# Start-up of a polynomial-attention and MLP kernel: batch 0's keys in three loads, constants, fillers and weight conversion in another order

## The chip, the cores and the metric

One core of a Trainium2 chip. The metric is the device time of one execution in microseconds (us), the median of the runs. The engines are TensorE (PE, with PEld for its weight loads), VectorE (DVE), ScalarE (ACT), GpSimd (POOL) and SyncE (SP), which only issues DMAs here.

## The reference

```
phi(x)  = outer(S1 x, S2 x), 8 x 8 features       # per batch, head and position
kv = sum over positions of phi(k) v ; z = sum over positions of phi(k)
attn = (phi(q) kv) / (phi(q) z + 1e-6)            # batch 4, 4 heads, 1088 positions, 32 wide
x = attn with the heads side by side              # 4 x 1088 rows of 128
xn = (x - mean(x)) / sqrt(var(x) + 1e-6) * g_ln
out = x + relu(xn W1) W2                          # W1 128 x 512, W2 512 x 128
```

q, k and v are float32. S1, S2, W1 and W2 arrive as float64, and the kernel turns them into float32 itself.

## The kernel before

The kernel's order is written out by hand: each engine works through its own queue in the order of the calls, and waits on semaphores for what it needs. The four batches pass through the stages keys (`turn_k`, `key_features`, `key_products`, `key_sums`, `key_scale`, `key_values`, `key_spread`), queries (`turn_q`, `query_features`, `query_rows`, `quotients`, `query_products`, `query_turn`), numerators (`numerators`, `columns_of`) and the MLP (`hidden`, `second`, `finish`, with `stats` and `root` for the norm), each batch's MLP under the next batch's attention. The rows of the output are in nine chunks; the first two are batch 0's halves.

The change is in the start-up, in which batch 0's first half passes alone while the weights are converted. These parts of it matter:

- **Loads.** `load_rows` (L94) issues one DMA on SP for a batch's keys or queries, 128 partitions with 34 positions of 32 floats each. SP's order at the start is S2, batch 0's keys (`kn`), queries (`qn`), W1, four loads of v, W2. VectorE's `turn_k(0, 0, 4, 0, 4)` turns the keys of the first four of nine position tiles of each group, two more calls the others.
- **Constants on GpSimd.** Ahead of everything: zeros in `vn` (L113), two iotas, the identity, `ident8` (L144), zeros in both `kT` (L148), -0.5 in `mhalf` (L150, the exponent of the norm's root), 1e-6 in `ac` (L155), zeros in `sq` (L159).
- **S.** L179 to L208: VectorE takes the float64 words of S1 and S2 apart and puts float32 together in `s_f`; `sketches` makes the projection matrices from it on TensorE.
- **Weight conversion.** Class `weight`: `split` (VectorE, L179 and L181, exponent and upper mantissa bits), `floats` on ScalarE (step 0 and 1: exponent, L242 and L244; step 2: mantissa, L246; step 3: low word, L248), `add` (GpSimd, L265, mantissa plus low word), `signed` (VectorE, L185), `last` (VectorE, L273, the product). For W2, `exps` (VectorE, L253 and L255) stands in place of steps 0 and 1. W1 is converted in halves of 256 columns; `split` writes both halves into the PSUM banks M[0] and M[2]. Each converted half goes through `mean_free` on TensorE, and a copy (L658 or L672) brings it back as `w1`.
- **Fillers.** `fill(n, bank, w)` (L161) has TensorE multiply ones by ones, n times w columns, with nothing that reads the result.

The order of the conversion among the rest, before:

```
W1.split(0, half); key_products ...; W1.split(half, half)
query_features(0, 0, 4) ... W1.floats ... quotients(0, 0, 4); key_values(0)
query_products, query_turn; W1.add(0, half); W1.add(half, half)
W1.signed(0, half); W1.last(dve, 0, half); W1.signed(half, half); W2.floats(3)
numerators(0, 0, 4); mean_free(0, M[0]); W1.last(dve, half, half)
turn_q(0, 4, 4); W2.split(); W2.exps(); W2.signed(); hidden(0, 0)
query_features(0, 4, 4); mean_free(half, FB); hidden(0, 1); W2.floats(2); W2.add()
query_rows(0, 4, 4); W2.last(dve); turn_k(1, ...)
```

Of the kernel before, what the change touches and what calls it, by code (L numbers as in the profile page):

```python
# [16 lines left out]
def _ap(t: bass.AP, p0: int, np_: int, off: int, free, step: int = 1):  # L17

    p = list(t.ap)[0]
    return bass.AP(  # L20
        t.tensor, t.offset + p0 * p[0] + off, [[p[0] * step, np_]] + [list(d) for d in free]
    )
# [3 lines left out]
def kernel(  # L26
# [20 lines left out]
    P = 128  # L47
# [24 lines left out]
    def const(shape, dtype, name):  # L72
        return consts.tile(shape, dtype, name=name)
# [17 lines left out]
    w1_raw = const([P, DH], moe_w_ch1.dtype, "w1_raw")  # L91
    w2_raw = const([P, JC * DM], moe_w_ch2.dtype, "w2_raw")

    def load_rows(dst, src, b):  # L94
        nc.sync.dma_start(
            out=dst[b],
            in_=bass.AP(src.tensor, src.offset + b * H * S * D, [[G * D, P], [1, G * D]]),
        )

    def load_v(b):  # L100
        base = v.offset + b * H * S * D
        for r in range(4):
# [4 lines left out]
                in_=bass.AP(v.tensor, base + NT * D * r, [[G * D, 32], [S * D, H], [1, n]]),  # L107
            )


    dve.memset(_ap(vn[0], 0, P, 7 * D, [[VH, H], [1, 2 * D]]), 0.0)
    for b in range(1, B):
        pool.memset(_ap(vn[b], 96, 32, 7 * D, [[VH, H], [1, 2 * D]]), 0.0)  # L113
    load_rows(kn, k, 0)
    load_rows(qn, q, 0)
    nc.sync.dma_start(out=w1_raw, in_=moe_w_ch1)
    load_v(0)
# [23 lines left out]
                      op0=ALU.logical_shift_right, op1=ALU.bitwise_and)  # L141
    dve.tensor_tensor(out=m8, in0=bit, in1=head, op=ALU.is_equal)
    ident8 = const([R2, P], F32, "ident8")
    pool.tensor_copy(out=_ap(ident8, 0, R2, 0, [[R, 16], [1, R]]),  # L144
                     in_=_ap(ident, 0, R2, R, [[0, 16], [1, R]]))
    kT = [const([P, NT * P], F32, f"kT{i}") for i in range(2)]
    for t in kT:
        pool.memset(t[:, 7 * P :], 0.0)  # L148
    mhalf = const([P, 4], F32, "mhalf")
    pool.memset(mhalf, -0.5)  # L150

    NE = R + 1
    acs = [const([P, 32 * NE], F32, f"ac{i}") for i in range(2)]
    for t in acs:
        pool.memset(_ap(t, 0, P, R, [[NE, 32]]), 1e-6)  # L155

    sq = [const([P, 32], F32, f"sq{b}") for b in range(B)]
    for t in sq:
        pool.memset(t, 0.0)  # L159

    def fill(n, bank, w=P):  # L161
        for _ in range(n):
            pe.matmul(bank[:, 0:w], ones, _ap(ones, 0, P, 0, [[0, w // P], [1, P]]),  # L163
                      start=True, stop=True)
# [52 lines left out]
    class weight:  # L217


        def __init__(self, dst, raw, tag, banks=None):  # L220
            self.dst, self.raw, self.plain = dst, raw, raw.dtype == F32
            self.banks = banks
            if not self.plain:
                self.t = exponent(raw, P, raw.shape[-1], tag)

        def cols(self, a, n):
            t = {k: x[:, a : a + n] for k, x in self.t.items()}
            if self.banks:

                y = self.banks[a // n].bitcast(U32)  # L230
                t["ex"], t["bits"] = y[:, 0:n], y[:, n : 2 * n]
            return t

# [38 lines left out]
                t = self.cols(a, n)  # L272
                eng.tensor_tensor(out=dst, in0=t["mant"], in1=t["e3"].bitcast(F32), op=ALU.mult)  # L273

    W1 = weight(w1g, w1_raw, "w1", banks=(M[0], M[2]))
    W2 = weight(w2, w2_raw, "w2")


# [14 lines left out]
    def sketches(y):  # L293

        pe.matmul(y[:, P : P + R2], s_f, ident[0:R2, 0:R2], start=True, stop=True)
        dve.tensor_tensor(
            out=_ap(sk, 0, P, 0, [[HR, 2], [R, H], [1, R]]),
            in0=_ap(y, 0, P, P, [[R, 2], [0, H], [1, R]]),
            in1=_ap(m32, 0, P, 0, [[0, 2], [1, H], [0, R]]),
            op=ALU.mult,  # L300
        )
        act.copy(sq[0][:, 0:R2], y[:, P : P + R2])
        for b in range(1, B):
            pool.tensor_copy(out=sq[b][:, 0:R2], in_=sq[0][:, 0:R2])

    def sketches2(y):

# [45 lines left out]
    def key_sums(b, y, o):  # L353
        f = fs[b % 2]
        for t in range(NT):
            c = t % 4
            pe.matmul(
                y[32 * c : 32 * c + 32, o : o + 32],
                f[:, KB + HR * t : KB + HR * (t + 1)],
                f[:, HR * t : HR * (t + 1)],  # L360
                start=(t < 4), stop=(t >= NT - 4),
            )
        (act.copy if b == 0 else dve.tensor_copy)(zT, y[:, o : o + H * R])
# [64 lines left out]
    def quotients(p, t0=0, n=8):  # L428
        m = n * H
        f, ac = fq[p], acs[p % 2]  # L430
        if t0 == 0:
            a2s[p] = small.tile([P, 32 * R], F32, tag="a2", name="a2")
        den = small.tile([P, 32], F32, tag="den", name="den")
        rden = small.tile([P, 32], F32, tag="rden", name="rden")
        a = _ap(f, 0, P, P * t0, [[32, m], [1, R]])
        dve.tensor_tensor(out=_ap(ac, 0, P, 0, [[NE, m], [1, R]]), in0=a,
                          in1=_ap(f, 0, P, P * t0 + R2, [[32, m], [1, R]]), op=ALU.mult)
        dve.tensor_reduce(out=den[:, 0:m], in_=_ap(ac, 0, P, 0, [[NE, m], [1, NE]]),
                          axis=AX.X, op=ALU.add)
        dve.reciprocal(rden[:, 0:m], den[:, 0:m])  # L440
        dve.tensor_tensor(out=_ap(a2s[p], 0, P, HR * t0, [[R, m], [1, R]]), in0=a,  # L441
                          in1=_ap(rden, 0, P, 0, [[1, m], [0, R]]), op=ALU.mult)
# [153 lines left out]
    def mean_free(a, bank):  # L596
        pe.matmul(bank[:, 0:half], cg, w1g[:, a : a + half], start=True, stop=True)
# [10 lines left out]
    turn_q(0, 0, 4)  # L608
    key_features(0, 4, 9, M[1])
    fill(1, X, 256)  # L610
    fill(1, X)
    key_sums(0, FB, 0)
    fill(1, X, 256)
    key_scale(0, FB, 32)
    W1.split(0, half)
    key_products(pool, 0, 4, 7)
    key_products(dve, 0, 7, 9, M[1], 4)
    W1.split(half, half)
    fill(1, X, 256)
    query_features(0, 0, 4)  # L620
    W1.floats(3, 0, half)
    query_rows(0, 0, 4)
    for step in (2, 0, 1):
        W1.floats(step, 0, half)
    pool.tensor_scalar(out=cg, in0=ident, scalar1=-1.0 / DM, scalar2=g_col,
                       op0=ALU.add, op1=ALU.mult)
    quotients(0, 0, 4)
    key_values(0)
    key_rows()
    W1.floats(2, half, half)  # L630
    fill(1, X, 256)
    fill(1, X)
    key_spread(0, M[1], 0)
    W1.floats(3, half, half)

    act.copy(kn[1][:, 0:1], a2s[0][:, 0:1])
    load_rows(kn, k, 1)
    load_rows(qn, q, 1)
    load_v(1)
    load_rows(kn, k, 2)  # L640
    query_products(0, pool, 2, 2)
    query_products(0, dve, 0, 2)
    query_turn(0, 0, 2)
    query_turn(0, 2, 2)
    W1.add(0, half)
    W1.add(half, half)
    W1.floats(0, half, half)
    W1.floats(1, half, half)
    W1.signed(0, half)
    W1.last(dve, 0, half)  # L650
    W1.signed(half, half)
    W2.floats(3)
    fill(2, X, 512)
    fill(1, X, 256)
    numerators(0, 0, 4)
    columns_of(0)
    mean_free(0, M[0])
    dve.tensor_copy(out=w1[:, 0:half], in_=M[0][:, 0:half])  # L658
    W1.last(dve, half, half)
    turn_q(0, 4, 4)  # L660
    W2.split()
    W2.exps()
    W2.signed()
    fill(1, M[1], 256)
# [2 lines left out]

    pool.memset(_ap(kT[0], 0, P, 7 * P + 96, [[P, 2], [1, 32]]), 0.0)
    hidden(0, 0)
    query_features(0, 4, 4)  # L670
    mean_free(half, FB)
    act.copy(w1[:, half:], FB[:, 0:half])  # L672
    hidden(0, 1)
    W2.floats(2)
    W2.add()
    query_rows(0, 4, 4)
    W2.last(dve)
    turn_k(1, 3, 4, 0, 7)
# [190 lines left out]
```

## Time and profile before

| | |
|---|---|
| runs | 113.71 us median of 3 (113.41 to 113.97) |
| profiled execution | 110.56 us, of which the span is 108.8 us |
| busy in the span | PE 101.8, PEld 69.2, DVE 71.9, ACT 39.0, POOL 50.3 us |
| DMA | 14.14 MB, mean 130 GB/s |

The profile is of one execution. Times in its rows are from the span's start; a group of instructions has its busy time, and the idle time of its engine ahead of it with what ended that. The matmuls' ends are modelled, and a busy TensorE is not TensorE at its peak.

### The profile page before, as it was taken

To read this page: it belongs to the slowest core of one execution; us is meant where nothing else is said; L and a number is where in the kernel's file an instruction comes from. 1 tells how busy PE (TensorE), PEld (TensorE's weight loads), DVE (VectorE), ACT (ScalarE), POOL (GpSimd) and SP (SyncE) were. 2 spreads that over 40 slices of the span, in tenths; PEclk is the share of its full clock that TensorE was granted. 3 is DMA by queue.
4 is the path that set the end of the run, shared out by engine and by line. 5 is a ranking of instruction groups with operands and counts; after the bars stand their busy time and mean duration, and the time that the engine had idled before them with its cause. 6 is when DMAs were issued, how large, how long until landed. Compare 5 with 4: busy or idle time off the path is not lost. (4 is left out here: it accounts for less than half of the span.)

```text
span 108.8 us, 3629 instructions
## 1 busy us (share of the span) xinstructions
PE 101.8 (94%) x1506; PEld 69.2 (64%) x1506; DVE 71.9 (66%) x209; ACT 39.0 (36%) x81; POOL 50.3 (46%) x64
## 2 busy tenths in 40 slices
PE   6989989987899999999999999999999999999890
PEld 3367737436783687836963786559449658759680
DVE  4689687929949948788879703896950593283410
ACT  5123882390223522434316601451282251071220
POOL 7339283042996497672950793069340034016000
PEclk9999999999999999999999999999999999999999
DMA  1997019960003595415496853430045440141031
GB/s 40 375 347 240 6 54 359 249 167 0 6 0 121 151 294 143 174 51 137 88 368 187 204 204 102 121 75 0 9 124 200 136 118 6 48 96 49 6 96 48
DMA packets 11763, 14.14 MB, mean 130 GB/s; under 512 B 2145, under 2 KB 8674, under 8 KB 11746
## 3 DMA queue, kind: packets, MB, share of 16 engines
q1 hardware_dynamic: 11584, 13.84, 41.9%
q8 instruction: 12, 0.20, 0.7%
q10 hardware_dynamic: 162, 0.07, 0.2%
q14 instruction: 5, 0.04, 0.1%
HBM read 9.70 MB, written 4.19 MB: 128 GB/s over the span
## 5 line engine op out<-in xcount | busy, mean ns | idle before, releaser
L568 PEld LDWEIGHTS M<-w,hT 128*128 128x128 f32 x256 | 31.0, 191 | 7.7 <-issue 3.8
L568 PE MATMUL M<-w,hT 128*128 128x128 f32 x256 | 34.3, 281 | 1.4 <-DVE w L273 1.3
L558 PE MATMUL M<-xT,w 128*128 128x512 f32 (+1 forms) x72 | 34.0, 586 | 0.5 <-DVE ob L580 0.5
L560 ACT ACTIVATE hT<-M 128x512 f32<-128x512 f32 (+1 forms) x36 | 20.6, 574 | 34.1 <-PE M L558 34.1
L448 POOL TENSOR_TENSOR qp<-a,fq 128x1024 f32<-128x1024 f32 (+1 forms) x9 | 16.2, 1812 | 22.3 <-DVE a L441 22.3
L580 DVE SCALAR_TENSOR_TENSOR ob<-M,rstd,x 128x128 f32<-128x128 f32 x32 | 9.0, 344 | 17.0 <-PE M L568 7.6
L558 PEld LDWEIGHTS M<-xT,w 128*128 128x128 f32 x72 | 12.0, 190 | 9.4 <-issue 6.1
L346 POOL TENSOR_TENSOR kp<-fs 128x1024 f32<-128x1024 f32 (+2 forms) x8 | 16.4, 2067 | 1.2 <-ACT fs L337 0.8
L459 DVE STREAM_TRANSPOSE qpT<-qp 128x1024 f32<-128x1024 f32 (+1 forms) x10 | 10.8, 1082 | 3.3 <-POOL qp L448 3.3
L163 PE MATMUL X<-ones 128*128 128x256 f32 (+2 forms) x24 | 10.3, 551 | 1.1 <-DVE ones L84 1.1
L542 POOL TENSOR_TENSOR rstd<-va,mhalf 128x4 f32<-128x4 f32 (+1 forms) x9 | 9.0, 1000 | 0.8
L540 POOL TENSOR_SCALAR va<-mv 128x4 f32<-128x4 f32 (+1 forms) x9 | 2.1, 229 | 15.3 <-DVE mv L533 15.0
L477 PE MATMUL X<-qpT,kvr 32*32 32x256 f32 (+2 forms) x384 | 7.5, 323 | 0.4 <-DVE qpT L459 0.4
L531 DVE BATCH_NORM_STATS2 st<-x 128x6 f32<-128x128 f32 x34 | 7.4, 280 | 0.3
L283 DVE STREAM_TRANSPOSE kT<-kn 128x224 f32<-128x224 f32 (+4 forms) x9 | 6.4, 755 | 0.8 <-DMA kn<-in_k_dram 0.8
L492 ACT COPY xT<-X 128x512 f32<-128x512 f32 (+1 forms) x8 | 4.2, 562 | 7.7 <-PE X L477 7.7
L425 DVE STREAM_TRANSPOSE fq<-X 128x512 f32<-128x512 f32 (+1 forms) x9 | 5.8, 670 | 1.7 <-PE X L415 1.6
L163 PEld LDWEIGHTS X<-ones 128*128 128x128 f32 x24 | 4.7, 221 | 3.4 <-issue 2.0
L477 PEld LDWEIGHTS X<-qpT,kvr 32*32 32x32 f32 x384 | 4.6, 103 | 3.3 <-issue 1.5
L374 PEld LDWEIGHTS FB<-kp,vn 128*32 128x32 f32 x288 | 4.2, 110 | 2.5 <-POOL kp L346 1.5
L265 POOL TENSOR_TENSOR mantw<-mantw,loww 128x256 f32<-128x256 f32 (+1 forms) x3 | 2.9, 996 | 5.9 <-ACT mantw L246 5.9
L523 DVE STREAM_TRANSPOSE x<-xx 128x512 f32<-128x512 f32 (+1 forms) x8 | 5.4, 670 | 0.5 <-DMA xx<-xd 0.4
(110 smaller groups left out, 89.1 us busy)
## 6 DMA issues: line engine op xcount, KB each, us to landing
kn<-in_k_dram SPq DMA_DIRECT2D x4, 544.0 KB, 4.1
qn<-in_q_dram SPq DMA_DIRECT2D x4, 544.0 KB, 5.1
out_dram<-ob SPq DMA_DIRECT2D x33, 64.0 KB, 1.8
xd<-xT SPq DMA_DIRECT2D x7, 256.0 KB, 2.1
xx<-xd SPq DMA_DIRECT2D x28, 64.0 KB, 1.9
vn<-in_v_dram SPq DMA_DIRECT2D x12, 144.0 KB, 5.4
w_raw<-in_moe_w_ch_dram SPq DMA_DIRECT2D x2, 512.0 KB, 5.8
vn<-in_v_dram SPq DMA_DIRECT2D x4, 112.0 KB, 3.7
```

The costliest lines, as they stand in the source:

```text
L163: pe.matmul(bank[:, 0:w], ones, _ap(ones, 0, P, 0, [[0, w // P], [1, P]]), start=True, stop=True)
L283: dve.transpose(_ap(kT[b % 2], 0, P, at + P * t0, dims), _ap(kn[b], 0, P, D * (NT * r0 + t0), [[D * NT, r1 - r0], [D, n], [1, D]]),)
L346: eng.tensor_tensor(out=_ap(o, 0, P, H * F * t0, [[F, (t1 - t0) * H], [R, R], [1, R]]), in0=_ap(a, 0, P, at, [[R, (t1 - t0) * H], [1, R], ...
L448: eng.tensor_tensor(out=_ap(qp[p, t0 // 4], 0, P, H * F * (t0 % 4), [[F, m], [R, R], [1, R]]), in0=_ap(a2s[p], 0, P, HR * t0, [[R, m], [1, ...
L459: dve.transpose(_ap(qpT[p], 0, P, 32 * t0, [[32, n], [width(p), 8], [1, 32]]), qp[p, t0 // 4][:, o : o + n * H * F],)
L477: pe.matmul(X[D * h : D * h + D, 512 * r + 32 * t0 : 512 * r + 32 * (t0 + n)], kvr[p if p < 4 else r][rows, DM * i + D * h : DM * i + D * ...
L531: dve.bn_stats(out=st[:, 6 * t : 6 * t + 6], in_=x[c][:, P * t : P * (t + 1)])
L542: pool.tensor_tensor(out=rs[:, 0:n], in0=va[:, 0:n], in1=mhalf[:, 0:n], op=ALU.pow)
L558: pe.matmul(hp[:, 0:n], w1[:, P * j : P * (j + 1)], xT[c][:, 0:n], start=True, stop=True)
L560: act.activation(_ap(hT[c], 0, P, 512 * j, dims), hp[:, 0:n], AF.Relu)
L568: pe.matmul(po[c][:, DM * t : DM * (t + 1)], hT[c][:, 512 * j + P * t : 512 * j + P * (t + 1)], w2[:, DM * j : DM * (j + 1)], start=(j == ...
L580: dve.scalar_tensor_tensor(out=ob[c][:, P * t : P * (t + 1)], in0=po[c][:, P * t : P * (t + 1)], scalar=rstd[c][:, t : t + 1], in1=x[c][:, ...
```

## The change

- Batch 0's keys come in three DMAs instead of one: positions 0 to 3 of each of four groups of nine (runs of 512 bytes), then positions 4 to 8 of the first three groups (640 bytes), then the last three positions of the fourth (384 bytes).
- GpSimd's constants: the zeros in `kT` shrink to the 32 columns per tile that stay unwritten, and come first; `ident8`, the zeros in `sq` (now 8 columns) and 1e-6 in `ac` come behind the copies of `sq` in `sketches`; `mhalf` and the zeros in `vn` come behind `key_spread(0, ...)`, ahead of the first query product. The sum of W1's first half moves up ahead of these.
- W1's second half: its split moves from ahead of the query rows to behind the first half's product, and writes to SBUF instead of bank M[2]; its steps on ScalarE come behind `columns_of(0)`, its signed step and its product behind W2's split.
- W2's mantissa on ScalarE and the sum on GpSimd move up ahead of the second hidden activation; on TensorE, `hidden(0, 1)` comes ahead of `mean_free(half, FB)`.
- Fillers: 256 columns ahead of `key_sums(0)` instead of 256 and 128, 128 instead of 256 behind it, 128 instead of 256 ahead of `query_features(0, 0, 4)`.

```diff
-    def load_rows(dst, src, b):
+    def load_rows(dst, src, b, at=0, parts=1, n=G):
+
+        dims = [[NT * D, parts], [1, D * n]]
         nc.sync.dma_start(
-            out=dst[b],
-            in_=bass.AP(src.tensor, src.offset + b * H * S * D, [[G * D, P], [1, G * D]]),
+            out=_ap(dst[b], 0, P, D * at, dims),
+            in_=bass.AP(src.tensor, src.offset + b * H * S * D + D * at, [[G * D, P]] + dims),
         )
...
+    kT = [const([P, NT * P], F32, f"kT{i}") for i in range(2)]
+    for t in kT:
+        pool.memset(_ap(t, 0, P, 7 * P + (3 if t is kT[0] else 96),
+                        [[P, 2], [4 if t is kT[0] else 1, 32]]), 0.0)
 
     dve.memset(_ap(vn[0], 0, P, 7 * D, [[VH, H], [1, 2 * D]]), 0.0)
-    for b in range(1, B):
-        pool.memset(_ap(vn[b], 96, 32, 7 * D, [[VH, H], [1, 2 * D]]), 0.0)
-    load_rows(kn, k, 0)
+    load_rows(kn, k, 0, 0, 4, 4)
+    load_rows(kn, k, 0, 4, 3, 5)
+    load_rows(kn, k, 0, 31, 1, 3)
     load_rows(qn, q, 0)
...
-    pool.tensor_copy(out=_ap(ident8, 0, R2, 0, [[R, 16], [1, R]]),
-                     in_=_ap(ident, 0, R2, R, [[0, 16], [1, R]]))
-    kT = [const([P, NT * P], F32, f"kT{i}") for i in range(2)]
-    for t in kT:
-        pool.memset(t[:, 7 * P :], 0.0)
     mhalf = const([P, 4], F32, "mhalf")
-    pool.memset(mhalf, -0.5)
...
-    for t in acs:
-        pool.memset(_ap(t, 0, P, R, [[NE, 32]]), 1e-6)
...
-    for t in sq:
-        pool.memset(t, 0.0)
...
-            if self.banks:
-
-                y = self.banks[a // n].bitcast(U32)
+            if self.bank is not None and a == 0:
+
+                y = self.bank.bitcast(U32)
                 t["ex"], t["bits"] = y[:, 0:n], y[:, n : 2 * n]
...
-    W1 = weight(w1g, w1_raw, "w1", banks=(M[0], M[2]))
+    W1 = weight(w1g, w1_raw, "w1", bank=M[0])
...
         for b in range(1, B):
             pool.tensor_copy(out=sq[b][:, 0:R2], in_=sq[0][:, 0:R2])
+
+        pool.tensor_copy(out=_ap(ident8, 0, R2, 0, [[R, 16], [1, R]]),
+                         in_=_ap(ident, 0, R2, R, [[0, 16], [1, R]]))
+        for t in sq:
+            pool.memset(t[:, R3:], 0.0)
+        for t in acs:
+            pool.memset(_ap(t, 0, P, R, [[NE, 32]]), 1e-6)
...
     key_features(0, 4, 9, M[1])
     fill(1, X, 256)
+    key_sums(0, FB, 0)
     fill(1, X)
-    key_sums(0, FB, 0)
-    fill(1, X, 256)
     key_scale(0, FB, 32)
     W1.split(0, half)
     key_products(pool, 0, 4, 7)
     key_products(dve, 0, 7, 9, M[1], 4)
-    W1.split(half, half)
-    fill(1, X, 256)
+    fill(1, X)
     query_features(0, 0, 4)
-    W1.floats(3, 0, half)
+    for step in (2, 3):
+        W1.floats(step, 0, half)
     query_rows(0, 0, 4)
-    for step in (2, 0, 1):
-        W1.floats(step, 0, half)
     pool.tensor_scalar(out=cg, in0=ident, scalar1=-1.0 / DM, scalar2=g_col,
                        op0=ALU.add, op1=ALU.mult)
+    W1.add(0, half)
+    for step in (0, 1):
+        W1.floats(step, 0, half)
     quotients(0, 0, 4)
     key_values(0)
     key_rows()
-    W1.floats(2, half, half)
+    W1.floats(3, half, half)
     fill(1, X, 256)
     fill(1, X)
     key_spread(0, M[1], 0)
-    W1.floats(3, half, half)
+    pool.memset(mhalf, -0.5)
+    for b in range(1, B):
+        pool.memset(_ap(vn[b], 96, 32, 7 * D, [[VH, H], [1, 2 * D]]), 0.0)
 
     act.copy(kn[1][:, 0:1], a2s[0][:, 0:1])
...
     load_rows(kn, k, 2)
+    W2.floats(3)
     query_products(0, pool, 2, 2)
     query_products(0, dve, 0, 2)
     query_turn(0, 0, 2)
     query_turn(0, 2, 2)
-    W1.add(0, half)
-    W1.add(half, half)
-    W1.floats(0, half, half)
-    W1.floats(1, half, half)
     W1.signed(0, half)
     W1.last(dve, 0, half)
-    W1.signed(half, half)
-    W2.floats(3)
+    W1.split(half, half)
     fill(2, X, 512)
     fill(1, X, 256)
     numerators(0, 0, 4)
     columns_of(0)
+    for step in (2, 0, 1):
+        W1.floats(step, half, half)
+    W1.add(half, half)
     mean_free(0, M[0])
     dve.tensor_copy(out=w1[:, 0:half], in_=M[0][:, 0:half])
-    W1.last(dve, half, half)
     turn_q(0, 4, 4)
     W2.split()
+    W1.signed(half, half)
+    W1.last(dve, half, half)
     W2.exps()
     W2.signed()
...
     hidden(0, 0)
+    W2.floats(2)
+    W2.add()
     query_features(0, 4, 4)
+    hidden(0, 1)
     mean_free(half, FB)
     act.copy(w1[:, half:], FB[:, 0:half])
-    hidden(0, 1)
-    W2.floats(2)
-    W2.add()
     query_rows(0, 4, 4)
```

More of the change, by code (lines that the diff above doesn't have):

```diff
@@ L217, with __init__ @@
     class weight:
-        def __init__(self, dst, raw, tag, banks=None):
+        def __init__(self, dst, raw, tag, bank=None):
             self.dst, self.raw, self.plain = dst, raw, raw.dtype == F32
-            self.banks = banks
+            self.bank = bank
             if not self.plain:
```

## The prediction

> **What bounds the kernel now.** I read the page first: TensorE is busy in nearly every slice, and the chain that ended last holds only the last 6 us. So the span is a steady, TensorE-paced stage behind a start-up, and a change to the start-up counts by how much earlier the steady stage begins.
>
> ```profile
> span 108.8 us, 3629 instructions
> PE   6989989987899999999999999999999999999890
> ```
>
> The second line is TensorE's busy tenths: 9s from slice 11 (about 27 us) to the tail. Next came the waits of the first 34 us (waiter, waited for, us, times, longest):
>
> ```profile
> PE M L568 <- DVE w L273: 1.3, 1, 1.3
> ```
>
> TensorE's longest stop in that stretch is 1.3 us, for VectorE's last product for W2. The timeline gives the chain there (start, duration, engine, line; in brackets the idle time before it and what ended it):
>
> ```profile
> 18.22 0.42 DVE L658 COPY w<-M 128x256 f32<-128x256 f32 x1 [0.46 <-PE M L597]
> 19.93 0.60 ACT L560 ACTIVATE hT<-M 128x512 f32<-128x512 f32 x1 [1.83 <-PE M L558]
> 20.16 0.42 DVE L253 TENSOR_SCALAR exfw<-exw 128x512 f32<-128x512 uint32 x1
> 21.07 0.69 DVE L185 SCALAR_TENSOR_TENSOR e3w<-w_raw,e2w 128x512 uint32<-128x512 uint32 x1
> 21.68 0.71 DVE L425 STREAM_TRANSPOSE fq<-X 128x512 f32<-128x512 f32 x1
> 22.34 0.71 ACT L246 ACTIVATE mantw<-bitsw,one 128x512 f32<-128x512 uint32 x1
> 23.13 1.27 POOL L265 TENSOR_TENSOR mantw<-mantw,loww 128x512 f32<-128x512 f32 x1 [5.89 <-ACT mantw L246]
> 24.43 0.69 DVE L273 TENSOR_TENSOR w<-mantw,e3w 128x512 f32<-128x512 f32 x1 [2.04 <-POOL mantw L265]
> 27.61 1.27 PE L331 MATMUL X<-sk,kT 128*64 128x64 f32 x36 [0.32 <-DVE kT L283]
> ```
>
> ScalarE's W2 mantissa (22.34) feeds GpSimd's sum (23.13), that W2's last product on VectorE (24.43, after 2.04 us of idling), and 3.18 us later the keys of batch 1 let TensorE go on (27.61). I take 24.43 as the clock of the start-up: what this product gains, the end gains, as long as TensorE's own queue allows.
>
> **The first keys and the constants behind S.** Rows of the start:
>
> ```profile
> 1.07 3.78 PE L163 MATMUL X<-ones 128*128 128x512 f32 x4 [1.07 <-DVE ones L84]
> 2.63 0.97 DVE L179 TENSOR_SCALAR exs<-s_raw 16x32 uint32<-16x32 uint32 x1
> 3.29 0.28 POOL L159 MEMSET sq<- 128x32 f32 x4
> 3.63 0.17 DVE L201 TENSOR_SCALAR exfs<-exs 16x32 f32<-16x32 uint32 x1
> 4.78 0.60 PE L295 MATMUL M<-ident,s_f 16*128 16x16 f32 x2
> 5.32 0.97 PE L163 MATMUL X<-ones 128*128 128x256 f32 x2
> 5.40 1.10 DVE L283 STREAM_TRANSPOSE kT<-kn 128x512 f32<-128x512 f32 x1 [0.76 <-DMA kn<-in_k_dram]
> 6.33 0.21 DVE L296 TENSOR_TENSOR sk<-M,m 128x64 f32<-128x64 f32 x1
> 6.60 0.69 PE L331 MATMUL M<-sk,kT 128*64 128x64 f32 x16 [0.31 <-DVE sk L296]
> ```
>
> S's first step takes 0.97 us where its like takes 0.17, and ends at 3.60, just behind GpSimd's last constant (3.57). With the constants moved behind S, VectorE may have S 0.97 - 0.17 = 0.8 us earlier. But the matmul of S (4.78) starts when the fillers before it end (1.07 + 3.78 = 4.85), and the filler behind it runs to 5.32 + 0.97 = 6.29. Neither filler changes. So the first key matmul comes from 6.60 to 6.29 at best: 0 to -0.31, however early S and the keys are. I take -0.31, for the keys have room: they must land by about 5.1 instead of 5.40 (transpose 0.93 until the next start, then 0.21), and the new first load has 512 of 1088 columns.
>
> The load becomes three issues instead of one, so qn, W1, v and W2 are queued two issues later on SP. W1 is the first that this could hurt:
>
> ```profile
> 2.05 0.43 SPq L116 DMA_DIRECT2D w_raw<-in_moe_w_ch_dram  x1
> DMA to landing us min/median/max: 6.0/6.0/6.0
> 8.90 0.40 DVE L179 TENSOR_SCALAR M<-w_raw 128x256 uint32<-128x256 uint32 x1
> ```
>
> Two issues of about 0.45 to 0.6 us put W1's at 3.0 to 3.25, while its read at 8.90 comes forward only 0.3 (the order up to there is unchanged otherwise). Behind that read lie two split steps of 0.4 and key products as wide as the query product below (0.69), 1.5 together, before VectorE is wanted at 10.8 (below), so W1 may come as late as 9.3. W1 landed at 2.05 + 6.0 = 8.05. I cost the loads at nothing and keep the late case as a rival.
>
> **The fillers.** Before, 256 + 128 columns stand ahead of key_sums (L357), 256 behind it and 256 ahead of the query features (L415); after, 256, 128 and 128.
>
> ```profile
> 8.50 0.92 PE L163 MATMUL X<-ones 128*128 128x256 f32 x4
> 9.35 0.38 PE L357 MATMUL FB<-fs 128*32 128x32 f32 x18
> 9.66 0.70 PE L163 MATMUL X<-ones 128*128 128x256 f32 x2
> 10.29 0.25 PE L367 MATMUL FB<-zT,s2b 128*32 128x8 f32 x8
> 11.10 0.50 PE L415 MATMUL X<-qT,sq 32*32 32x128 f32 x32
> 11.78 0.72 DVE L425 STREAM_TRANSPOSE fq<-X 128x512 f32<-128x512 f32 x1 [0.63 <-PE X L415]
> ```
>
> 384 columns hold TensorE for 9.35 - 8.50 = 0.85, 256 for 10.29 - 9.66 = 0.63: 128 are worth 0.22. Three times that is -0.66 (not less than -0.3, if ScalarE's small copies between these matmuls become the limit). With -0.31, the query features reach VectorE at 11.78 - 0.97 = 10.8. W1's second split (two steps of 0.4) leaves VectorE ahead of this row and brings nothing here: VectorE waited 0.63 for TensorE anyway.
>
> **GpSimd's queue in the quotients.** Into the stretch in which GpSimd stood idle before the query product go one W1 sum, the constant for the root and three memsets of v.
>
> ```profile
> 0.72 0.80 POOL L113 MEMSET vn<- 32x256 f32 x3 [0.29 <-POOLq L853]
> 11.21 0.37 POOL L625 TENSOR_SCALAR cg<-ident,g_col 128x128 f32<-128x128 f32 x1
> 13.56 0.29 DVE L441 TENSOR_TENSOR a<-fq,rden 128x128 f32<-128x128 f32 x1
> 13.88 0.69 DVE L448 TENSOR_TENSOR qp<-a,fq 128x512 f32<-128x512 f32 x1
> 13.93 1.57 POOL L448 TENSOR_TENSOR qp<-a,fq 128x512 f32<-128x512 f32 x1 [2.35 <-DVE a L441]
> 26.64 1.95 POOL L448 TENSOR_TENSOR qp<-a,fq 128x1024 f32<-128x1024 f32 x1 [2.25 <-DVE a L441]
> 16.66 0.77 DVE L273 TENSOR_TENSOR w1g<-mantw,e3w 128x256 f32<-128x256 f32 x1
> 18.56 0.42 DVE L273 TENSOR_TENSOR w1g<-mantw,e3w 128x256 f32<-128x256 f32 x1
> ```
>
> The query rows and quotients took from 11.78 to 13.56 + 0.29 = 13.85, that is 2.07, and would now take from 10.8 to 12.87. cg moves with the key products by 0.3 and ends at 11.28; the sum (half of the 1.27 for twice the columns, 0.64) runs to 11.9, the memsets with the root's constant (0.9) to 12.8. The query product would find GpSimd free just in time. But two-input work of both engines does not overlap here: GpSimd's 512-wide product took 1.57 beside VectorE's 0.69, where 1.95 for 1024 makes 0.98, so it waited about 0.6; and W1's product on VectorE took 0.77 beside GpSimd's sum and 0.42 without. The quotients' first product, due at 11.55, so waits until 11.9: +0.35. Sum: 11.78 - 0.97 + 0.35, that is -0.6 for the quotients, the query products and the W1 copy (18.22 to 17.6). The two splits of W1's second half now stand ahead of that copy; one signed step (0.4, an estimate: the 0.69 of twice the width, less the fixed part) leaves there, and VectorE idled 0.46 there: 0.8 of work into 0.86 of room, cost 0 to 0.4, taken at 0.
>
> **W1's second half and W2's mantissa.** From the copy on, VectorE's order is query transpose, W2's split, W1's signed step and product, W2's exponents, its signed step, the query rows, W2's product. The W1 product stood between the copy and the exponents before too, so only the signed step is new there: exponents at 20.16 - 0.6 + 0.4 = 19.95, signed step 0.91 later at 20.9, rows 0.61 later at 21.5, W2's product 0.71 later at 22.25. ScalarE now does the mantissa right behind the first hidden activation (19.93 - 0.6 + 0.60, so 19.95 to 20.65), and GpSimd's sum is ready to start at 20.65. Before, it ran while VectorE stood still; now it meets the exponents and the signed step. Taking turns, as in the rows above, it gets in before the signed step, from 20.9 to 22.2; all behind it is 1.27 later, and W2's product starts at 23.5. Against 24.43 that is -0.9. If the sum gets in only behind the signed step, 20.9 + 0.69 + 1.27 = 22.9 (-1.5); without any blocking, 22.3 (-2.1). TensorE's queue allows this: its lead there is the 0.97 above and the idle 1.3 and 0.32, together 2.6.
>
> [...]
>
> **The sum.** -0.9 of a span of 108.8 gives 107.9. The profiled execution took 110.56 (span and 1.76 around it); the runs' median is 113.71, 3.15 above it, and I carry the difference over: 112.8.
>
> **The rivals.**
> - No blocking: VectorE and GpSimd overlap freely in these places. Then the +0.35 goes too: -2.1 - 0.35 = -2.45, 111.3. For: the two stretched rows are a few, and something else may have stretched them (the product's 1.57 is one instruction). Against: two stretched rows that fit one reading to 0.1 us. Chance 0.25.
> - GpSimd's constants hold the quotients as they held S: VectorE would get on only at 12.8, when GpSimd's queue is through. The quotients proper (2.07 less the 0.72 of the query rows) then end at 12.8 + 1.35 = 14.15, where 13.85 stands before; from there +0.3 instead of -0.6, and W2's product at 23.5 + 0.9 = 24.4. Nothing is left: 113.7. For: 0.97 against 0.17. [...] Chance 0.17.
> - Slower, by the loads. The keys now go in runs of 512, 640 and 384 bytes instead of whole rows. The 512-byte fetches later in the kernel moved like this (columns: stretch, its length, busy and count of PE, PEld, DVE, ACT, POOL, then TensorE's clock, DMA share, GB/s):
>
> ```profile
> 35.00:35.50 0.50, 0.50 (x34) 0.48 (x37) 0.43 (x3) 0.37 (x1) 0.00 (x0) 1.00 0.46 131
> GB/s 40 375 347 240 6 54 359 249 167 0 6 0 121 151 294 143 174 51 137 88 368 187 204 204 102 121 75 0 9 124 200 136 118 6 48 96 49 6 96 48
> ```
>
> The second line is the page's rate by slices of 2.7 us: 375 GB/s in the slice in which the keys came, so 557 KB took 1.5 us; at 131 GB/s they take 4.25. Everything behind comes 2.75 later, W1 at 10.8. Its split and the products (1.5) end at 12.3, the query rows start there instead of at 10.8, and W2's product comes at 23.5 + 1.5 = 25.0: +0.6, 114.3. It decides from W1 at 10.2, where the 0.9 is used up. Against: the DMA share in that row is 0.46, so it was short of issues, not of engines. Chance 0.13.
>
> **How the numbers follow.** Main case 0.45, no blocking 0.25, nothing left 0.17, slower 0.13. What tells a change from none here is about 0.5%, 0.57 us. Faster: the main case but for 0.07 of it, and all of the first rival, 0.63. Same: those 0.07 and 0.14 of the second rival, 0.21. Slower: the loads and the rest of the second, 0.16. The range goes from 111.2 (no blocking, full gain) to 113.9 (nothing left, with the runs' own spread of 0.25) and leaves out the slow loads and a little at each end. The main case alone: 112.1 to 113.3.
>
> **What would show it.** Right: the first key matmul at 6.3 and not earlier although VectorE has S some 0.8 earlier; the query rows at about 10.8; a quotient's or W2 exponent's step two or three times its former length beside a GpSimd sum; W2's product at 23 to 24, the batch-1 keys on TensorE near 26.7. Wrong: W1's first split waiting for its DMA beyond 9.3; W2's product before 22.6 (no blocking) or at 24.4; or a wait on TensorE behind 27 us that was not there before and gives the gain back.

## The result, and the profile after

The changed kernel takes 110.69 us (median of 20 executions, 109.25 to 113.61), the kernel before 110.98 us (20 executions, 110.49 to 114.62). Forecast were 112.8 us in a range of 111.2 to 113.9, and 113.71 was the base. The times of both kernels fall into two groups, and in the changed kernel's profiles the two differ in when TensorE comes to its full rate. Ratios compare the executions within 1.5% of each kernel's fastest, here the early groups and the 112.0 of before: changed to before 0.9884, 95% interval [0.9855, 0.9913], about -1.3 us.

| | early group, median | late group, median | others |
|---|---|---|---|
| before | 110.67 us (11 up to 111.1) | 113.83 us (7) | 112.0, 112.61 |
| changed | 109.36 us (10 up to 110.1) | 113.37 us (9) | 111.27 |

The three executions that the prediction took as its base, 113.41 to 113.97, lie in the late group of before; the execution whose profile it read, 110.56, in the early one.

The changed kernel was profiled twice. One profile is early: an execution of 109.7 us, in the slower half of its group. From its page:

```profile
span 107.8 us, 3627 instructions
PE   6999979978999999999999999999999999999880
```

Before, the span was 108.8. The waits of its first 34 us:

```profile
PE M L571 <- DVE w L269: 0.5, 1, 0.5
```

TensorE's stop for W2's last product, 1.3 us before, is down to 0.5. The timeline of the same profile:

```profile
2.57 0.17 DVE L175 TENSOR_SCALAR exs<-s_raw 16x32 uint32<-16x32 uint32 x1 [0.56 <-DMA s_raw<-in_S_dram]
4.78 0.61 PE L291 MATMUL M<-ident,s_f 16*128 16x16 f32 x2
5.31 1.18 PE L159 MATMUL X<-ones 128*128 128x256 f32 x2
6.42 0.69 PE L334 MATMUL M<-sk,kT 128*64 128x64 f32 x16
8.32 0.70 PE L159 MATMUL X<-ones 128*128 128x256 f32 x2
8.88 0.43 DVE L175 TENSOR_SCALAR M<-w_raw 128x256 uint32<-128x256 uint32 x1
9.26 0.49 PE L159 MATMUL X<-ones 128*128 128x128 f32 x2
10.96 0.72 DVE L428 STREAM_TRANSPOSE fq<-X 128x512 f32<-128x512 f32 x1 [0.60 <-PE X L418]
11.36 0.73 POOL L261 TENSOR_TENSOR mantw<-mantw,loww 128x256 f32<-128x256 f32 x1
11.71 0.53 DVE L439 TENSOR_TENSOR ac<-fq 128x128 f32<-128x128 f32 x1
17.53 0.42 DVE L662 COPY w<-M 128x256 f32<-128x256 f32 x1 [0.70 <-PE M L600]
20.20 0.42 DVE L249 TENSOR_SCALAR exfw<-exw 128x512 f32<-128x512 uint32 x1
20.52 1.26 POOL L261 TENSOR_TENSOR mantw<-mantw,loww 128x512 f32<-128x512 f32 x1 [1.72 <-ACT mantw L242]
20.65 1.42 DVE L251 TENSOR_SCALAR e2w<-exfw 128x512 uint32<-128x512 f32 x1
22.10 0.69 DVE L181 SCALAR_TENSOR_TENSOR e3w<-w_raw,e2w 128x512 uint32<-128x512 uint32 x1
23.34 0.65 DVE L269 TENSOR_TENSOR w<-mantw,e3w 128x512 f32<-128x512 f32 x1
26.48 1.27 PE L334 MATMUL X<-sk,kT 128*64 128x64 f32 x36 [0.32 <-DVE kT L279]
```

S's first step is down to 0.17 us and its matmul still starts at 4.78. The query rows start at 10.96, GpSimd's two sums stand beside stretched VectorE steps (0.53 at 11.71, where it was 0.29; 1.42 at 20.65, where it was 0.43), W2's product starts at 23.34 and the keys of batch 1 at 26.48.

The other profile of the changed kernel is late: 113.37 us, span 111.6. Its timeline:

```profile
5.32 1.22 PE L159 MATMUL X<-ones 128*128 128x256 f32 x2
6.47 1.12 PE L334 MATMUL M<-sk,kT 128*64 128x64 f32 x16
8.51 1.33 PE L334 MATMUL M<-sk,kT 128*64 128x64 f32 x20
9.78 1.22 PE L159 MATMUL X<-ones 128*128 128x256 f32 x2
11.39 0.80 PE L159 MATMUL X<-ones 128*128 128x128 f32 x2
13.99 0.72 DVE L428 STREAM_TRANSPOSE fq<-X 128x512 f32<-128x512 f32 x1 [2.89 <-PE X L418]
17.46 2.31 PE L159 MATMUL X<-ones 128*128 128x512 f32 x6
27.25 0.65 DVE L269 TENSOR_TENSOR w<-mantw,e3w 128x512 f32<-128x512 f32 x1
30.39 1.27 PE L334 MATMUL X<-sk,kT 128*64 128x64 f32 x36 [0.32 <-DVE kT L279]
```

The same 256 filler columns take 1.22 us where the early profile has 0.70, the first 16 key matmuls 1.12 instead of 0.69. Only from about 17 us on are the rows as in the early profile (2.31 for 1,280 columns). The keys of batch 1 come 30.39 - 26.48 = 3.91 later, the span ends 3.8 later: the whole difference arises in the start-up. The granted clock does not show it. Here is the row of the late profile for 5 to 9 us (stretch, its length, busy time and count of PE, PEld, DVE, ACT and POOL, then the granted clock, DMA share and GB/s):

```profile
5.00:9.00 4.00, 4.00 (x34) 3.13 (x35) 1.70 (x5) 0.70 (x3) 1.89 (x11) 1.00 0.96 333
```

The clock stands at 1.00 and TensorE counts as busy throughout, while its instructions take nearly twice as long.

### The profile page after: what moved, and what is told of

Read it like the earlier page. It is cut to its first block, busy times and chain, and to the rows that moved or that the text cites. A ratio compares the mean times of both kernels' runs of the same rounds, so it can differ in the third digit from the quotient of the medians.

```text
span 111.6 us, 3627 instructions
## 1 busy us (share of the span) xinstructions
PE 106.0 (95%) x1504; PEld 72.2 (65%) x1504; DVE 71.5 (64%) x209; ACT 39.1 (35%) x81; POOL 49.7 (45%) x64
## 5 line engine op out<-in xcount | busy, mean ns | idle before, releaser
L451 POOL TENSOR_TENSOR qp<-a,fq 128x1024 f32<-128x1024 f32 (+1 forms) x9 | 16.1, 1804 | 22.6 <-DVE a L444 22.6
L159 PE MATMUL X<-ones 128*128 128x512 f32 (+2 forms) x22 | 11.7, 664 | 1.1 <-DVE ones L84 1.1
L159 PEld LDWEIGHTS X<-ones 128*128 128x128 f32 x22 | 5.4, 283 | 3.7 <-issue 2.0
L377 PEld LDWEIGHTS FB<-kp,vn 128*32 128x32 f32 x288 | 5.1, 126 | 2.7 <-POOL kp L349 1.5
L377 PE MATMUL FB<-kp,vn 128*32 128x64 f32 x288 | 5.8, 244 | 0.0
## 6 DMA issues: line engine op xcount, KB each, us to landing
vn<-in_v_dram SPq DMA_DIRECT2D x4, 112.0 KB, 5.2
```

Of the source, the lines that this page charges most:

```text
L377: pe.matmul(FB[D * h : D * h + D, 64 : 64 + F], vn[b][:, VH * h + D * t : VH * h + D * (t + 1)], kp[b % 2][:, H * F * t + F * h : H * F * ...
L451: eng.tensor_tensor(out=_ap(qp[p, t0 // 4], 0, P, H * F * (t0 % 4), [[F, m], [R, R], [1, R]]), in0=_ap(a2s[p], 0, P, HR * t0, [[R, m], [1, ...
```

## The experiments

Theory: the steps of the start-up are as predicted, and TensorE's rate alone makes the late group. Rivals: the late executions lose their time outside the span or by something else; the steps only happen to add up. First the changed kernel runs again, and one part at a time is undone.

**The changed kernel again** (no edit).

> The changed kernel once more, for a profile in which TensorE runs at full rate from about 7 us on, as it did in the profile of before (in the first profile of the changed kernel a 256-column filler still took 1.22 us at 9.8 us, and the full rate came at about 17 us). Theory: ratio 0.988 again, the span 107.4. First key matmul near 6.3, query rows near 10.8, W2's second exponent step stretched to about 1.4 us by GpSimd's sum, W2's product near 23.4, batch 1's keys on TensorE near 26.3. Rival (no blocking by GpSimd): exponent steps 0.42 each and W2's product before 22.6.

Measured: 0.9904 [0.9863, 0.9946]; 109.39 to 109.79 us in six of twelve executions, 110.67 in one, 113.29 to 113.71 in five. Its profile is the early one above.

**Batch 0's keys in one load again.**

```
-    load_rows(kn, k, 0, 0, 4, 4); (kn, k, 0, 4, 3, 5); (kn, k, 0, 31, 1, 3)
+    load_rows(kn, k, 0)
```

> The changed kernel with batch 0's keys in one load, as before. Theory (fillers bind the first key matmul): 0.3 us slower than the changed kernel, ratio to before 0.991, first key matmul at 6.6. Rival (three loads delay what is queued behind them): faster than the changed kernel by 0.3 us or more, ratio below 0.986, with W1's split no longer waiting. Second rival (the load hides anyway): 0.988.

Measured: 0.9943 [0.9907, 0.998]. Four of twelve executions are early, 109.72 to 109.82, where the changed kernel's above are 109.39 to 109.79; three lie at 111.02 to 112.22, five at 113.53 to 113.84. The profiled execution took 112.22. Its timeline:

```profile
5.10 0.70 PE L157 MATMUL X<-ones 128*128 128x256 f32 x2
5.73 1.08 DVE L277 STREAM_TRANSPOSE kT<-kn 128x512 f32<-128x512 f32 x1 [2.16 <-DMA kn<-in_k_dram]
6.92 0.69 PE L332 MATMUL M<-sk,kT 128*64 128x64 f32 x16 [1.12 <-DVE sk L290]
8.22 1.33 PE L332 MATMUL M<-sk,kT 128*64 128x64 f32 x20
9.48 1.22 PE L157 MATMUL X<-ones 128*128 128x256 f32 x2
15.28 0.92 PE L157 MATMUL X<-ones 128*128 128x256 f32 x4
```

and the granted clock on its page, in slices of 2.76 us:

```profile
PEclk9995579999999999999999999999999999999999
```

Here TensorE is at full rate by 5.10. VectorE waits for the one long load and turns the keys at 5.73, where the changed kernel's early profile does so at 4.21; S's projection stands behind that in VectorE's queue, so TensorE stops 1.12 us. It is at half rate again from 8.2 to about 15. The loss of a rate once reached shows in the granted clock (5, 5 and 7 tenths from 8.3 to 16.6); a full rate that has not come yet, as in the late profile above, does not. The split of the keys takes that stop away: in both profiles of the changed kernel TensorE does not stop ahead of the first key matmul. The clocks of all executions point the same way, though they do not show that the stop is what loses the rate: with the keys in one load 5 of 12 have a mean granted clock of 0.984 or less, of the unchanged kernel before beside them 7 of 23, of the changed kernel 2 of 32 (both 0.984; one is the 111.27 between its groups). These counts suggest that the split does more than the 0.3 us that was expected of it.

**The fillers of before put back** (384 columns more).

```
     fill(1, X, 256)
+    fill(1, X)
     key_sums(0, FB, 0)
-    fill(1, X)
+    fill(1, X, 256)
     key_scale(0, FB, 32)
...
-    fill(1, X)
+    fill(1, X, 256)
     query_features(0, 0, 4)
```

> The changed kernel with the fillers around key_sums and the query features as before (384 columns more). Theory: 0.66 us slower at the query rows and 0.5 to 0.66 us at the end, ratio 0.993 to 0.994. Rival (the fillers only cover waits): no change, 0.988.

Measured: 0.9874 [0.9848, 0.9901], 109.02 to 109.62 and one of 113.27: by the times the cut is worth nothing, against the theory. From the profile (span 107.8):

```profile
5.31 0.80 PE L159 MATMUL X<-ones 128*128 128x256 f32 x2
6.04 0.69 PE L334 MATMUL M<-sk,kT 128*64 128x64 f32 x16
11.23 0.72 DVE L428 STREAM_TRANSPOSE fq<-X 128x512 f32<-128x512 f32 x1 [1.07 <-PE X L418]
```

The first key matmul stands at 6.04, not 6.42, though the order ahead of it is the changed kernel's: the filler took 0.80 instead of 1.18, so the full rate came earlier in this execution. From there to the query rows it takes 5.19 us, the changed kernel 4.54. So the cut gives 0.65 within the kernel. Of that, 0.18 is lost behind it (table below), because GpSimd's W1 sum here runs ahead of the quotients' first product (11.00 to 11.74, the product at 11.98), which takes 0.29 instead of 0.53. In this execution the earlier start makes up for the rest; that it does so in the other four early ones is not shown. What the cut is worth at the end of the changed kernel stays open.

**W2's mantissa, sum and the second hidden block in the order of before.**

```
     hidden(0, 0)
-    W2.floats(2); W2.add()
     query_features(0, 4, 4)
-    hidden(0, 1)
     mean_free(half, FB); act.copy(w1[:, half:], FB[:, 0:half])
+    hidden(0, 1)
+    W2.floats(2); W2.add()
     query_rows(0, 4, 4)
```

> The changed kernel with W2's mantissa and sum behind the second hidden activation and mean_free ahead of that, as before. Theory (GpSimd's sum blocks VectorE, so the early sum gains only part): W2's product 0.6 to 1.0 us later than in the changed kernel, VectorE waiting for it again; ratio 0.994 to 0.998. Rival (the early sum is worth its whole 2 us): ratio above 1.003. Second rival (TensorE's queue sets the end, not this product): 0.988.

Measured: 110.21 once, 112.5 to 114.69 in the five others, no usable ratio. Its profile is late, so it stands beside the changed kernel's late one:

```profile
24.41 0.43 DVE L251 TENSOR_SCALAR e2w<-exfw 128x512 uint32<-128x512 f32 x1
26.97 1.27 POOL L261 TENSOR_TENSOR mantw<-mantw,loww 128x512 f32<-128x512 f32 x1 [4.41 <-ACT mantw L242]
28.27 0.69 DVE L269 TENSOR_TENSOR w<-mantw,e3w 128x512 f32<-128x512 f32 x1 [2.07 <-POOL mantw L261]
```

The query rows stand at 13.99 in both. The exponent step is undisturbed (0.43), and W2's product comes at 28.27 instead of 27.25, after 2.07 us of waiting for the sum. Spans: 112.7 and 111.6. The earlier sum, with the hidden block moved along with it, gives 1.0 us, although it stretches a step by 1.0.

**The kernel before with its first filler cut**, from 1,024 to 128 columns: does the dense start bring the full rate?

```
-    fill(2, X, 512)
+    fill(1, X)
     turn_k(0, 0, 4, 0, 4)
```

> The kernel before with its first filler cut from 2 x 512 columns to 128. Theory (the times near 113.7 us are executions in which TensorE keeps half rate until about 17 us because its early work was not dense for long enough; the ones near 110.6 have the full rate from about 6 us): with the filler gone the early full rate is not reached, all runs come out near 113.5 or above, and the profile shows a 256-column filler at 1.2 us instead of 0.7 as late as 10 us. Rival (the two groups of times come from something else, the loads for instance): runs near 110.6 stay as frequent as before, or all become faster by up to 0.1 because S is no longer held by the filler.

Measured: 1.0229 [1.0162, 1.0297], 113.09 to 115.33 us in all seven executions; that ratio sets late executions against early ones, since there was no early one: without the dense start the full rate never came early. In the profile the fillers are still at half rate at 13:

```profile
11.94 1.22 PE L163 MATMUL X<-ones 128*128 128x256 f32 x2
13.32 1.22 PE L163 MATMUL X<-ones 128*128 128x256 f32 x2
```

**768 filler columns instead of 256 ahead of the first key matmul**, in the changed kernel and then in the kernel before.

```
-    fill(1, X, 256)
+    fill(2, X, 384)
     key_features(0, 0, 4, M[0])
```

> The changed kernel with 768 instead of 256 filler columns ahead of the first key matmul. Theory: the early dense stretch is 0.85 to 1.7 us longer, so fewer executions keep half rate (one in four or less near 114 instead of about half), and the ones at full rate are 0.4 to 1.3 us slower than the changed kernel, 109.7 to 110.6; ratio 0.992 to 1.0. Rival (the rate has nothing to do with the filler): half of the runs stay late.

> The kernel before, with 768 filler columns instead of 256 ahead of the first key matmul. Theory (what separates 110.5-110.9 us from 113.4-114.6 us in the kernel before is whether TensorE reaches full rate at about 6 us or at about 17 us): no run above 112 us, all at 110.6 to 111.8 us, of which up to 0.9 us is paid for 512 more columns; ratio against early runs of the kernel before 1.000 to 1.010; a filler of 256 columns takes 0.70 us from about 7 us on. Rival (the late times come from outside the span or from something other than TensorE's rate): runs at 113.4 us and above go on in about a third of the executions.

Measured, changed: 0.9922 [0.9879, 0.9965], all twelve executions 109.38 to 110.83. Before: 1.0024 [1.0001, 1.0047], all twelve 110.74 to 112.22; of the 30 executions of the unchanged kernel before on the same chip, 12 took 113.4 us or more. The late group is gone from both kernels. So it is TensorE's rate that makes it, and 512 more dense columns behind 5.3 us prevent it. Why these columns do what the key matmuls do not is not shown, for the late execution above counts TensorE busy there too. The full rate comes within the filler in both profiles. The changed kernel's:

```profile
5.32 1.74 PE L159 MATMUL X<-ones 128*128 128x384 f32 x4
```

The kernel before, in an execution of 112.22, the slowest of its twelve:

```profile
5.31 2.47 PE L163 MATMUL X<-ones 128*128 128x384 f32 x4
9.61 0.92 PE L163 MATMUL X<-ones 128*128 128x256 f32 x4
```

An estimate from the rows shown (1.22 and 0.70 for 256 columns, 3.78 for 1,024 at half rate, 2.31 for 1,280 at full) gives 768 columns 2.9 us at half rate and 1.5 at full. So 1.74 is nearly all at full rate, 2.47 mostly at half.

**W2's sum on VectorE, behind its signed step.**

```
     W2.floats(2)
-    W2.add()
...
+    W2.add(dve)
     query_rows(0, 4, 4)
```

> The changed kernel with the sum of W2's mantissa and low word on VectorE (behind the signed step) instead of GpSimd. Theory (GpSimd's sum blocks VectorE's second exponent step for 1.0 us): the exponent steps are 0.42 each again, the sum costs VectorE 0.7, W2's product comes 0.3 us earlier, ratio 0.985 against 0.988. Rival (no blocking, VectorE is simply full): 0.7 us later, ratio 0.994.

Measured: 0.9815 [0.9753, 0.9878], 108.27 to 109.37 and one of 112.88. Timeline:

```profile
5.05 0.70 PE L159 MATMUL X<-ones 128*128 128x256 f32 x2
8.93 0.43 DVE L175 TENSOR_SCALAR M<-w_raw 128x256 uint32<-128x256 uint32 x1 [0.67 <-DMA w_raw<-in_moe_w_ch_dram]
19.56 0.42 DVE L249 TENSOR_SCALAR exfw<-exw 128x512 f32<-128x512 uint32 x1
20.01 0.43 DVE L251 TENSOR_SCALAR e2w<-exfw 128x512 uint32<-128x512 f32 x1
21.08 0.68 DVE L261 TENSOR_TENSOR mantw<-mantw,loww 128x512 f32<-128x512 f32 x1
22.32 0.65 DVE L269 TENSOR_TENSOR w<-mantw,e3w 128x512 f32<-128x512 f32 x1
```

Without GpSimd's sum beside it the exponent step is back at 0.43, and the sum costs VectorE 0.68 instead: W2's product comes 11.99 behind the query rows instead of 12.38. The blocking cost 1.0, and 0.4 of it can be had at that product; the rest of this span is 0.2 longer (table below).

**GpSimd's constants in front of S again** (the added lines behind S and behind the quotients go back to their places of before).

> The changed kernel with all of GpSimd's constants in front again, as before. Theory (S waits for the filler on TensorE, not for GpSimd): S's first step takes 0.9 us again and S ends 0.7 to 1.0 us later, but its matmul stays at 4.78 and the first key matmul moves by at most 0.1; the quotients' first product is still beside the W1 sum; nothing at the end, 0.986 to 0.990. Rival (the constants were part of the gain): 0.3 us or more slower, ratio above 0.991.

Measured: 0.9873 [0.9813, 0.9932], 109.18 to 110.13 and one of 113.91. The start in its profile:

```profile
2.63 0.97 DVE L183 TENSOR_SCALAR exs<-s_raw 16x32 uint32<-16x32 uint32 x1
8.49 0.71 DVE L407 STREAM_TRANSPOSE qT<-qn 128x512 f32<-128x512 f32 x1 [0.61 <-DMA qn<-in_q_dram]
9.77 0.43 DVE L183 TENSOR_SCALAR M<-w_raw 128x256 uint32<-128x256 uint32 x1 [0.57 <-DMA w_raw<-in_moe_w_ch_dram]
```

S's step is at 0.97 again, and S's matmul stays at 4.78: the constants' move is worth nothing that the ratio shows (0.9873 against 0.9884). The other two rows show the loads late in this execution.

**The kernel before with only the changed kernel's fillers** (the third diff above, its signs reversed).

> The kernel before with only the changed kernel's shorter fillers (384 columns fewer between the first key matmul and the query rows). Theory (the cut is worth 3 x 0.22 us where the first half of W1 lands at 8.05 us, and is eaten in the changed kernel because W1 lands at 8.7 us or later there): query rows 0.5 to 0.7 us earlier than in the kernel before after the same first key matmul, 110.0 to 110.4 us, ratio 0.993 to 0.996. Rival (VectorE's steps set the query rows in both kernels, so that a filler's cut is worth nothing): ratio 0.998 to 1.002.

Measured: 0.9989 [0.994, 1.0039], which decides nothing, for it mixes two things: three executions took 110.05 to 110.15, four lay between 111.3 and 112.6, five at 113.79 or more. The three are quicker than each of the 30 executions of the unchanged kernel before on the same chip (110.52 and up). In the profile (110.06 us) the query rows come 4.54 behind the first key matmul instead of 5.18, and the span is 108.3 instead of 108.8: the cut works in the kernel before too, -0.64 at the query rows and -0.5 at the end. On the other side 5 of the 12 have a granted clock of 0.984 or less, of the unchanged kernel 4 of 30 (0.985 or less): with fewer fillers the rate seems to be lost more often, though so few executions do not show it.

**The first queries loaded in parts**, the half turned first ahead of W1, the rest in two loads behind W2.

```
-    load_rows(qn, q, 0)
+    load_q(0, [[8 * D, 4], [1, 4 * D]])
     nc.sync.dma_start(out=w1_raw, in_=moe_w_ch1)
...
+    load_q(4 * D, [[8 * D, 3], [1, 4 * D]])
+    load_q(28 * D, [[1, 6 * D]])
```

> The changed kernel with the first queries loaded in parts: the half that is turned first ahead of W1, the rest in two loads behind W2's. Theory (W1's first half lands at 8.7 to 10.0 us because three key loads and the whole query load stand ahead of it, and its readers wait for it): it lands 0.4 to 0.8 us earlier, the wait of 0.3 to 0.7 us ahead of VectorE's read of W1 goes, 108.8 to 109.5 us, ratio 0.982 to 0.987. Rival (the read of W1 is not on the path that sets the end, or the two further loads delay V by as much): as the changed kernel, ratio 0.987 to 0.991.

Measured: 0.9846 [0.9815, 0.9878], 108.79 to 109.62 and one of 113.68. The wait for W1 is gone from the profile (its read comes 2.31 behind the first key matmul, as in the kernel before), but the query rows come 4.55 behind it, as without the edit. By the ratios the edit gives 0.4 to 0.6 us, and the profiled execution, the slowest of the five early ones, shows no step that gave it; that stays open.

**All three together**: W2's sum on VectorE, the queries in parts, the long filler.

> The changed kernel with W2's sum on VectorE, the first queries loaded in parts, and 768 filler columns instead of 256 ahead of the first key matmul. Theory: the long filler keeps every run at full rate from about 7 us (no run above 112 us), the sum on VectorE is worth 0.3 to 0.7 us, the query load in parts up to 0.5 us: 108.4 to 109.4 us, ratio 0.979 to 0.988, and the lowest median of all runs together. Rival (the long filler costs its 0.5 to 0.9 us on the path, and the loads give nothing back): 109.4 to 110.0 us, ratio 0.988 to 0.993.

Measured: 0.9926 [0.9888, 0.9963], 109.39 to 110.9 in all twelve, median 110.17: below both kernels (110.69 and 110.98) and without a late execution, but not the 108.4 to 109.4 of the theory. The rival's price of the filler was nearer, and by the times the two other parts add nothing to the long filler, which alone has 0.9922 and a median of 109.95 (on another chip); the profile, of the quickest of the twelve, does have W2's product 12.00 behind the query rows, as with the sum on VectorE alone. The two other parts alone have lower medians still (109.0 and 109.1 of six each), with one late execution each.

## Why the prediction was right or wrong

Of the profiles at full rate, the starts of the rows (us), and the distances between them, which no longer contain the moment at which the rate came:

| kernel | first key matmul | to W1's read | to query rows | from there to W2's product | on to batch-1 keys | on to the end |
|---|---|---|---|---|---|---|
| before | 6.60 | 2.30 | 5.18 | 12.65 | 3.18 | 81.2 |
| changed | 6.42 | 2.46 | 4.54 | 12.38 | 3.14 | 81.3 |
| changed, old fillers | 6.04 | 2.64 | 5.19 | 12.20 | 3.14 | 81.2 |
| changed, long filler | 6.99 | 3.00 | 4.54 | 12.40 | 3.14 | 81.2 |
| changed, W2's sum on VectorE | 5.68 | 3.25 | 4.65 | 11.99 | 3.13 | 81.6 |
| changed, constants in front | 6.12 | 3.65 | 5.05 | 12.40 | 3.13 | 81.5 |
| changed, queries in parts | 6.00 | 2.31 | 4.55 | 12.39 | 3.13 | 81.7 |
| before, new fillers | 6.75 | 2.30 | 4.54 | 12.64 | 3.18 | 81.2 |

- **First keys and constants: the limit held, its size did not.** S's matmul did not move, as said, and the filler behind it is what the first key matmul waits for. But the prediction took that filler at a fixed 0.97 and called 6.29 "at best". The filler takes 0.70, 0.80 and 1.18 us in three early profiles with the same order up to there, and 1.22 in the late ones, by when TensorE's rate rises; the first key matmul stands at 5.68, 6.04 and 6.42 in these three, at 6.47 in two late ones. In the kernel before, the two early profiles with the short filler have it at 6.60 and 6.75, where TensorE waits 0.31 and 0.48 for VectorE. So by these profiles the loads bring the first key matmul forward by 0.2 to 0.9 us, as the rate comes; 0.31 is one value between.
- **Fillers: held at the query rows.** Forecast -0.66, measured -0.64 (5.18 to 4.54) in the kernel before and -0.65 (5.19 to 4.54) in the changed one. At the end of the changed kernel no time shows it.
- **Loads: held, with the bound.** W1's read waited for its load in four of the six changed profiles of the table, and the prediction's 9.3 against a first key matmul at 6.29 allows it 3.0 behind that matmul. At 3.00 it cost nothing, at 3.25 0.1, and at 3.65 0.5. The slow loads of the rival happen in part, at a tenth to a half of a microsecond, not at 1.5.
- **GpSimd's queue in the quotients: held.** The quotients' first product was stretched by 0.24 (0.53 instead of 0.29), where +0.35 was taken, and the W1 copy came at 17.53 (17.6 forecast).
- **W2: held in size and kind, with another step blocked.** The exponents began at 20.20 (19.95), the blocked step was the second exponent and not the signed one, the signed step began at 22.10 (22.2), W2's product at 23.34 (23.5), batch 1's keys at 26.48 (26.7). The way from the query rows to that product is a little shorter than forecast, 12.38 instead of 12.7. The second exponent took 1.42 beside GpSimd's sum (20.52 to 21.78) and 0.43 without it, in the kernel before and with the sum on VectorE. That the two engines take turns was the author's estimate from the rows of 1.57 and 0.77; why the step is longer beside the sum, no run shows.
- **The sum of the steps: held in one execution, and there in part by luck.** A span of 107.9 was forecast, 107.8 measured; 107.9 and the 1.76 around it make 109.7, the time of that execution. The first key matmul gave less than forecast there (0.18), the way to W2's product more (0.27), and the two balance. Over the whole early group the gain is about 1.3 us (110.67 to 109.36), not 0.9. A first key matmul that mostly comes earlier than 6.42 would explain that, but no profile of a typical early execution of the changed kernel shows it.
- **Wrong: "I carry the difference over: 112.8".** The 3.15 us between the profiled execution and the three runs was no constant lying around the span, but the late group. Of the executions of before beside the later experiments, one of 113.69 us has a span of 111.9 and one of 110.72 a span of 108.9, so what lies around the span stays at 1.8. The changed kernel's profiles show where inside the span the time goes: first key matmuls and fillers at half rate until about 17 us. With the profiled execution as base the same -0.9 gives 109.7, and the early executions took 109.25 to 110.1. Of the changed kernel's executions half were early and the rest late, so the median of 20 fell between the groups, where it says little: 110.69, with 10 executions up to 110.1 and 9 from 113.3 on. Against the late executions alone the forecast is not far off (113.37 measured, 112.8 forecast), but there the change is worth only 113.83 - 113.37 = 0.46 us; which of the steps are hidden at half rate was not tried. One reading of the prediction is off without harm: TensorE's tenths are all 9s from about 30 us on, not 27.

The no-blocking rival (W2's product before 22.6) and the one in which the constants hold the quotients (24.4) are both refuted by 23.34.

## What to carry to other kernels

Where a profiled execution is some per cent quicker than the runs around it, first ask at which rate of TensorE its start ran: compare like instructions early and late in the span (a filler of 256 columns at 1.22 or 0.70 us) before a difference is added as a constant. In a start-up, measure distances from a row behind the moment at which TensorE's rate rises, for comparisons of whole times mix that moment in. And before shortening fillers, ask whether they are what brings the rate: 512 more columns took the late group away from both kernels at 0.2 to 0.4 us by the ratios, 896 fewer at the start of the kernel before made all seven executions late, some 3 us above its early ones.

## What the runs showed of the hardware

TensorE at the start runs at half rate: the first 1,024 filler columns take 3.78 us in both profiles of the changed kernel, 1,280 from 17.46 on take 2.31. With one and the same program the full rate comes before about 6.5 us in one execution and at about 17 us in the next (the first 16 key matmuls take 0.69 us at 6.42 in the one, 1.12 at 6.47 in the other; 256 filler columns at 8.32 take 0.70 us in the one, at 9.78 they take 1.22 in the other). It goes with the dense columns at the start: with 768 instead of 256 ahead of the first key matmul none of 24 executions of the two kernels was late, with 128 instead of 1,024 in the first filler all seven of the kernel before were. Between the two profiles of the changed kernel the late rate makes 3.8 of 111.6 us, 3.4%. Why the late executions need until 17 us, and what decides in which execution the rate comes early, no run settles.

The granted clock of the records shows 1.00 while the full rate has not come yet (late profile, 5 to 9 us), and 0.5 when it has been lost again (0.50 from 9 to 13 us, keys in one load): instruction lengths tell more of a start-up than that row does. The lost rate seems to come in steps. Mean clocks of 0.984, 0.969 and 0.954 stand over spans of 109.5, 110.4 and 111.7 us (changed kernel, and the same with its keys in one load). At half rate that makes about 3.5, 6.8 and 10.3 us, an estimate from the missing clock and the span; in the one profile of the middle kind the rows show half rate from 8.2 to about 15.
